# q and k of a fused attention and MLP-mixer kernel: transposes by DMA in place of transposes by TensorE

## The chip, the cores and the metric

The kernel runs on one core of a Trainium2 chip. The metric is the device time of one execution in microseconds (us), as the median of several runs. The kernel before takes 470.36 us (three runs, 468.58 to 470.69). A "slow" state of a run is kept apart; it appeared three times, in one run of the kernel before (635.32 us) and in two runs of e12_q_only, and these runs are in no comparison.

## The reference

The inputs are 8 batches of 12 heads, 448 rows, 64 columns. Attention with normalized q and k is followed by an MLP mixer over the 768 columns of all heads. Cut to what matters:

```python
q_n = q / (norm(q, axis=-1) + 1e-6)
k_n = k / (norm(k, axis=-1) + 1e-6)
attn = softmax(q_n @ k_n.T / tau)             # tau = 0.1
x = (attn @ v)  ->  (batch, 448, 768)
h = relu(x.T @ w_tok1) @ w_tok2               # mixes the 448 rows, 256 hidden
u = x + h.T
out = u + relu(u @ w_ch1) @ w_ch2             # mixes the 768 columns, 1536 hidden
```

## The kernel before

Two heads are one pair, so there are 48 pairs; three pairs are a half batch, which is what one set of loads of q, k and v brings. `scaled` divides q and k by their norms and writes them in fp16 as `qn` and `kn`, 112 partitions by 512 elements. The score matmul takes q and k with the 64 columns on the partitions (64x448 in its trace), so they are transposed first: `tpose` does it with 8 TensorE transposes into PSUM (to which this kernel's matmuls write) and one VectorE copy to `qk`.

The scores go to `psS`, a large PSUM tile with a single buffer (`ps2`, `bufs=1`); all other PSUM tiles share the four slots of pool `ps`. A pair has two score groups, 0 and 1, and ScalarE computes the exponential of each. So each score group waits until the exponential of the group before it has read `psS`. TensorE fills the time between score groups with mixer matmuls of the batch before (`feed`).

```python
ps  = ctx.enter_context(tc.tile_pool(name="ps",  bufs=4, space=PSUM))
ps2 = ctx.enter_context(tc.tile_pool(name="ps2", bufs=1, space=PSUM))
att = ctx.enter_context(tc.tile_pool(name="att", bufs=3))
# ... cut ...
    def load_qk(n, lo=0, hi=6):
        # ... cut: tiles qh, kh, vs of half n ...
        nc.sync.dma_start(out=half[n]["q"][...], in_=q[...])
        nc.sync.dma_start(out=half[n]["k"][...], in_=k[...])

    def scaled(i, dve_k=False):
        lo = 2 * NCH * (i % HP)
        for a, (nm, src) in enumerate(zip(("qn", "kn"), sides(i))):
            dst = pipe[i][nm] = att.tile([SC, NCH, 2, E], FP16, name=f"{nm}_{i}", tag=nm)
            eng = nc.vector if dve_k and a else nc.gpsimd
            # ... cut: dst = src * rn ...

    def tpose(i):
        st = pipe[i]
        pst = ps.tile([128, 2, NCH, SC], FP16, name=f"pst_{i}", tag="b")
        for a, src in enumerate((st["qn"], st["kn"])):
            for c in range(NCH):
                nc.tensor.transpose(pst[:, a, c, :], src[:, c], id16[:SC, :SC])
        qk = att.tile([128, 2, S], FP16, name=f"qk_{i}", tag="qk")
        nc.vector.tensor_copy(out=qk[:], in_=pst[:].rearrange("p a c s -> p a (c s)"))
        st["qk"] = qk

    def score(i, cg):
        # ... cut ...
        psS = ps2.tile([SC, 2, 2, 512], FP32, name=f"psS_{i}_{cg}", tag="s")
        for j in range(2):
            c = 2 * cg + j
            for hh in range(2):
                hb = hh * 64
                nc.tensor.matmul(psS[:, hh, j, 0:S], qk[hb:hb + 64, 1, c * SC:(c + 1) * SC],
                                 qk[hb:hb + 64, 0, :], start=True, stop=True)
        nc.scalar.activation(out=st["pt"][:, cg], in_=psS[:, :, :, 0:S], func=AF.Exp, scale=inv_tau)
# ... cut; the loop over the pairs:
        for i in range(NP_ALL + 1):
            # ... cut: loads, squares ...
            if i >= 4 and i + 2 < NP_ALL:
                scaled(i + 2)
            # ... cut ...
                if i:
                    score(i, 0)
                feed(quota * 0.3)
                if i:
                    pv(i - 1, 0)
                feed(quota * 0.2, 500.0)
                if i and i + 1 < NP_ALL:
                    tpose(i + 1)
                if i:
                    score(i, 1)
                feed(quota * 0.3)
                if i:
                    pv(i - 1, 1)
                feed(quota * 0.2)
```

The traces keep the order of these calls: on TensorE, in the kernel before, 47 of the 48 pairs have their transposes between the two score groups of one pair, where `tpose` is called (the first pair's come ahead of all scores).

## Time and profile before

| | before |
|---|---|
| time, median of 3 runs | 470.36 us |
| TensorE busy in the profiled run | 418.2 us of 468.7 |
| start-up, until the first mixer matmul | 69.0 us |
| mixer part, until the last score matmul | 333.5 us, TensorE idle 7.1 |
| rest | 66.2 us |

The stages in the table are read from the profile's busy times; the first lines are its page. The line of part 1 gives busy time, share of the span and instruction count by engine. In part 2 each digit is the busy share of one of 40 equal slices in tenths; PEclk is the TensorE clock that the throttle granted, also in tenths. The last line is part 4, the chain of work that ended last, by engine.

```profile
PE 418.2 (89%) x4136; PEld 257.6 (55%) x4136; DVE 219.1 (47%) x442; ACT 232.4 (50%) x262; POOL 219.0 (47%) x220
...
PE   0405879999999999999999999999999999999995
...
PEclk9999999999999999999999999999999999999999
DMA  9997999941496037630585056811200011001012
...
PE 84%; ACT 6%; DVE 4%; POOL 2%; issue 2%; DMA 1%; SPq 0%; ACTq 0%; POOLq 0%
```

After the start-up TensorE is at 9 in nearly every slice, its clock is full (0.99 or 1.00 in the stages below), and it holds 84% of the chain. In the start-up the PEclk row must not be trusted: the trace's clock records begin at 61.8 us, and the profile prints full clock where it has none. Until then one 65-column matmul of `psO` starts 55 ns after the one before it (median), and 32 ns in what is recorded as full clock; in the recorded half clock it is 55 ns too. So the start-up had the pace of half clock.

The busy times of the three stages of the kernel before follow. The columns are the window, its length, then busy time and instruction count of PE, PEld, DVE, ACT and POOL, then the mean granted TensorE clock, the DMA engines' busy share, and GB/s.

```profile
0.00:69.00 69.00, 30.70 (x317) 20.24 (x318) 37.37 (x64) 28.38 (x31) 51.93 (x60) 1.00 1.04 208
69.00:402.50 333.50, 326.38 (x3386) 200.86 (x3386) 170.25 (x355) 187.66 (x203) 167.05 (x161) 1.00 0.41 99
402.50:468.70 66.20, 61.13 (x436) 36.45 (x434) 11.44 (x23) 16.33 (x30) 0.00 (x0) 0.99 0.11 42
```

In the start-up the DMA engines are saturated (a busy share of 1.04, 208 GB/s), and TensorE, busy for 30.7 of 69 us, is not the limit.

A stretch of the timeline of the kernel before shows one pair in the mixer part. The columns are start, duration, engine, line, operation and tiles; a bracket at the end is the idle time before it and what released it.

```profile
202.23 0.36 PE L183 MATMUL pst_2758<-id_86,qn_2594 112*128 112x112 f16 x4
202.43 0.36 PE L183 MATMUL pst_2758<-id_86,kn_2596 112*128 112x112 f16 x4
202.43 0.54 ACT L261 ACTIVATE gt_1_2351<-psG_6_2750 128x448 f16<-128x448 f32 x1
...
202.82 0.62 DVE L185 COPY qk_2767<-pst_2758 128x896 f16<-128x896 f16 x1 [0.89 <-PE pst_2758 L183]
...
203.34 1.66 ACT L200 ACTIVATE pt_2723<-psS_1_2769 112x1792 f16<-112x1792 f32 x1 [0.37 <-PE psS_1_2769 L198]
...
205.06 0.58 PE L198 MATMUL psS_0_2815<-qk_2767 64*112 64x448 f16 x4 [1.14 <-ACT pt_2723 L200]
```

The eight transposes cost TensorE about half a microsecond (from the first one's start to the next matmul 0.49), the copy costs VectorE 0.62. The second exponential starts right after its score, the first score group of the next pair waits for this exponential (not for the transposes, which were done at 203.4), and TensorE loses 1.1 us. This pair is one of the worst: the waits of TensorE in the kernel before begin like this (waiting tile, what it waited for, us in total, times, longest):

```profile
PE pst_145 L183 <- POOL qn_141 L175: 11.7, 1, 11.7
PE psS_1_290 L198 <- ACT pt_251 L200: 10.6, 1, 10.6
...
PE psS_0_2815 L198 <- ACT pt_2723 L200: 1.1, 1, 1.1
```

The two long ones are in the start-up.

### The profile page before, as it was taken

The page shows a single profiled execution, that of the slowest core. Times are in us where ns is not written, and L with a number is a line of the kernel's source. Part 1 is how long each engine was busy: PE and PEld are TensorE (multiplying, and loading weights), DVE is VectorE, ACT ScalarE, POOL GpSimd, SP SyncE. Part 2 cuts the span into 40 slices and gives each one's busy share as a digit, 9 for nine tenths or more (in the row PEclk, how much of TensorE's full clock was granted, in tenths as well). Part 3 has the DMA queues.
Part 4 walks back from the last instruction along what each step waited for, and adds up shares of the span by engine and source line. Part 5 has one row for each costly group of instructions (what it writes and reads, how often), then busy time and mean ns, then how long its engine had stood idle before and what let it go on. Part 6 is the DMA issues. An engine that isn't in the chain of part 4 may idle for free.

```text
span 468.7 us, 9522 instructions
## 1 busy us (share of the span) xinstructions
PE 418.2 (89%) x4136; PEld 257.6 (55%) x4136; DVE 219.1 (47%) x442; ACT 232.4 (50%) x262; POOL 219.0 (47%) x220
## 2 busy tenths in 40 slices
PE   0405879999999999999999999999999999999995
PEld 0203546655655566656665666555655666556563
DVE  2448658455654455354645455445635343123000
ACT  2324664776457634675457543674467433520410
POOL 4599698586455644465283825373481300000000
PEclk9999999999999999999999999999999999999999
DMA  9997999941496037630585056811200011001012
GB/s 193 229 229 182 216 205 230 214 93 28 123 216 119 1 106 174 144 69 4 141 196 119 0 143 138 182 31 50 79 35 1 19 51 44 26 22 48 34 49 86
DMA packets 72841, 50.02 MB, mean 107 GB/s; under 512 B 44448, under 2 KB 68448, under 8 KB 72800
## 3 DMA queue, kind: packets, MB, share of 16 engines
q1 hardware_dynamic: 69408, 44.05, 39.7%
q0 software_dynamic: 3392, 5.37, 6.2%
q8 instruction: 32, 0.52, 0.5%
q14 instruction: 9, 0.07, 0.1%
HBM read 43.78 MB, written 11.01 MB: 117 GB/s over the span
## 4 chain that ended last, share of the span: by engine, by line
PE 84%; ACT 6%; DVE 4%; POOL 2%; issue 2%; DMA 1%; SPq 0%; ACTq 0%; POOLq 0%
DMA qh_105<-in_q_dram 1%; DVE kn_324 L175 1%; DVE ssq_118 L157 1%; ACT pt_630 L200 1%; ACT pt_482 L200 1%; ACT pt_1042 L200 1%; DVE ssq_126 L157 0%; POOL sq_207 L152 0%; PE psF_2_1_5429 L278 0%; PE psF_2_0_5377 L278 0%; PE psF_2_1_4787 L278 0%; PE psF_1_0_4581 L278 0%; PE psF_0_1_4513 L278 0%; PE psF_2_1_3968 L278 0%; PE psF_2_0_3897 L278 0%
## 5 line engine op out<-in xcount | busy, mean ns | idle before, releaser
L259 PEld LDWEIGHTS <-wc1t 128*128 128x128 f16 x576 | 51.5, 98 | 51.1 <-issue 9.8
L278 PEld LDWEIGHTS <-gt_2_3862 128*128 128x128 f16 x168 | 15.3, 98 | 12.5 <-issue 2.4
L278 PEld LDWEIGHTS <-gt_1_2351 128*128 128x128 f16 x168 | 15.4, 98 | 12.2 <-issue 2.4
L278 PEld LDWEIGHTS <-gt_0_804 128*128 128x128 f16 x168 | 15.5, 98 | 11.2 <-issue 1.4
L278 PEld LDWEIGHTS <-gt_3_5342 128*128 128x128 f16 x168 | 15.9, 98 | 9.6
L227 PEld LDWEIGHTS <-w1t 128*128 128x128 f16 x128 | 11.3, 100 | 8.6 <-issue 3.5
L183 PE MATMUL pst_145<-id_86,qn_141 112*128 112x112 f16 x4 | 0.6, 294 | 11.7 <-POOL qn_141 L175 11.7
L198 PE MATMUL psS_1_290<-qk_185 64*112 64x448 f16 x4 | 1.0, 574 | 10.6 <-ACT pt_251 L200 10.6
L198 PEld LDWEIGHTS <-qk_185 64*112 64x112 f16 x8 | 0.8, 176 | 13.0 <-issue 12.5
L284 DVE COPY ost_0_6031<-psF_0_0_6032 128x384 f32<-128x384 f32 x1 | 0.6, 558 | 15.2 <-PE psF_0_0_6032 L281 15.2
L164 ACT ACTIVATE rn_119<-ssq_118,tiny 112x16 f32<-112x16 f32 x3 | 0.9, 307 | 12.1 <-DVE ssq_118 L157 12.1
L183 PEld LDWEIGHTS <-qn_141 112*128 112x128 f16 x4 | 0.3, 129 | 11.6 <-POOL qn_141 L175 11.6
L175 POOL TENSOR_TENSOR qn_5044<-qh_4311,rn_4315 112x512 f16<-112x512 f32 x1 | 1.0, 1042 | 10.4 <-DVE rn_4315 L167 10.4
L164 ACT ACTIVATE rn_109<-ssq_108,tiny 112x16 f32<-112x16 f32 x3 | 0.9, 304 | 9.2 <-DVE ssq_108 L157 9.2
L175 DVE TENSOR_TENSOR kn_324<-kh_116,rn_119 112x512 f16<-112x512 f32 x1 | 4.7, 4685 | 0.0
L281 PEld LDWEIGHTS <-ut_3_5341 128*128 128x128 f16 x42 | 3.5, 98 | 1.8
L281 PEld LDWEIGHTS <-ut_0_803 128*128 128x128 f16 x42 | 3.5, 98 | 1.8
L281 PEld LDWEIGHTS <-ut_1_2350 128*128 128x128 f16 x42 | 3.5, 98 | 1.8
L281 PEld LDWEIGHTS <-ut_2_3861 128*128 128x128 f16 x42 | 3.5, 98 | 1.8
L175 POOL TENSOR_TENSOR qn_3954<-qh_3191,rn_3195 112x512 f16<-112x512 f32 x1 | 1.0, 1043 | 7.3 <-DVE rn_3195 L167 7.3
L198 PE MATMUL psS_0_400<-qk_365 64*112 64x448 f16 x4 | 1.0, 598 | 3.7 <-DVE qk_365 L185 3.7
L152 POOL TENSOR_TENSOR sq_2301<-qh_2033 112x512 f32<-112x512 f32 x1 | 1.0, 1041 | 6.9 <-DVE ssq_1701 L157 6.9
(1726 smaller groups left out, 1310.3 us busy)
## 6 DMA issues: line engine op xcount, KB each, us to landing
wc1t<-in_moe_w_ch_dram POOLq DMA_DIRECT2D x2, 1152.0 KB, 13.2
wc2t<-in_moe_w_ch_dram POOLq DMA_DIRECT2D x2, 1152.0 KB, 15.3
vs_107<-in_v_dram SPq DMA_DIRECT2D x1, 672.0 KB, 8.3
qh_115<-in_q_dram SPq DMA_DIRECT2D x1, 672.0 KB, 10.6
kh_116<-in_k_dram SPq DMA_DIRECT2D x1, 672.0 KB, 12.6
vs_117<-in_v_dram SPq DMA_DIRECT2D x1, 672.0 KB, 8.6
qh_123<-in_q_dram SPq DMA_DIRECT2D x1, 672.0 KB, 11.1
kh_124<-in_k_dram SPq DMA_DIRECT2D x1, 672.0 KB, 13.1
```

What stands on the lines that cost most here:

```text
L152: nc.gpsimd.tensor_mul(out=sq[:, a], in0=src, in1=src)
L157: nc.vector.tensor_reduce(out=half[i // HP]["ssq"][:, :, lo:lo + 2 * NCH], in_=pipe[i]["sq"][:], axis=AXX.X, op=ALU.add)
L164: nc.scalar.activation(out=rn, in_=ssq, func=AF.Ln, bias=tiny[:])
L175: eng.tensor_tensor(out=dst[:].rearrange("p c g e -> p g c e"), in0=src, in1=_bcast_free(rn, E), op=ALU.mult)
L183: nc.tensor.transpose(pst[:, a, c, :], src[:, c], id16[:SC, :SC])
L198: nc.tensor.matmul(psS[:, hh, j, 0:S], qk[hb:hb + 64, 1, c * SC:(c + 1) * SC], qk[hb:hb + 64, 0, :], start=True, stop=True)
L200: nc.scalar.activation(out=st["pt"][:, cg], in_=psS[:, :, :, 0:S], func=AF.Exp, scale=inv_tau)
L227: nc.tensor.matmul(psR[:], w1t[:, m, tt * 128:(tt + 1) * 128], x16[b][:, m, dh * DH:(dh + 1) * DH], start=(m == 0), stop=(m == 3))
L259: nc.tensor.matmul(psG[:], wc1t[:, dt, ct * 128:(ct + 1) * 128], ut[:, dt, span(b)], start=(dt == 0), stop=(dt == DT - 1))
L278: nc.tensor.matmul(psF[:], rows(gt, ct), wc2t[:, ct, dh * DH:(dh + 1) * DH], start=(ct == 0), stop=False)
L281: nc.tensor.matmul(psF[:, 128 * i:128 * (i + 1)], rows(ut, 3 * dh + i), id16[:], start=False, stop=(i == 2))
L284: nc.vector.tensor_copy(out=o[:, 0:DH], in_=psF[:])
```

## The change

The intent is to take 384 transposes off the busiest engine and 48 copies off VectorE. Each pair's q and k are transposed by one DMA transpose each, from SBUF to SBUF, issued on ScalarE's queue at the place of the old `tpose`. This is the whole diff:

```diff
     def tpose(i):
         st = pipe[i]
-        pst = ps.tile([128, 2, NCH, SC], FP16, name=f"pst_{i}", tag="b")
+        qk = att.tile([128, 2, S], FP16, name=f"qk_{i}", tag="qk")
         for a, src in enumerate((st["qn"], st["kn"])):
-            for c in range(NCH):
-                nc.tensor.transpose(pst[:, a, c, :], src[:, c], id16[:SC, :SC])
-        qk = att.tile([128, 2, S], FP16, name=f"qk_{i}", tag="qk")
-        nc.vector.tensor_copy(out=qk[:], in_=pst[:].rearrange("p a c s -> p a (c s)"))
+            nc.scalar.dma_start_transpose(out=qk[:, a].rearrange("p (c s) -> p c s", c=NCH),
+                                          in_=src[:].rearrange("p c g e -> p (c g e)"))
         st["qk"] = qk
```

Nothing else moves: on ScalarE the two issues stand between the exponential of score group 0 and that of score group 1 of the pair before.

## The prediction

> **What bounds the kernel now.** TensorE. The busy row gives PE 89%, ScalarE 50%, VectorE 47%. By stages: 0 to 69 us is a start-up in which PE is busy only 31 of 69 us and the DMA engines are saturated (GB/s row: about 210); from 69 to 416 us PE is busy 340 of 347 us and DMA 40%; then 53 us of output matmuls. The chain of waits is 84% PE.
>
> **What the change removes.** Per pair 8 transposes. In the timeline the next matmul starts 0.49 us after the first transpose, so about 0.45 us of PE per pair once the clock is up: 48 pairs make about 20 us, nearly all on the PE-bound path in the middle. Also 48 VectorE copies of 0.62 us (30 us), off the path, and one PSUM slot per pair.
>
> **What it adds.** 96 DMA transposes of 112x512 f16 (11 MB), issued in order on ScalarE between the first and second exponential of each pair. [...]
>
> **How much is on the path.** For the 42 pairs from 60 us on I read from the timeline the time between ScalarE being free for the issues and the next pair's first score matmul, which needs q and k transposed. It is 2.1 us in about nine pairs, 3.6 to 4.4 in most, up to 7.4. [...]29 of 42 pairs stall, together about 42 us. The second exponential, held up by 2 us, has 1.3 us of slack on average, and none in some 13 pairs where score and exponential already alternate; that is the same stall. Against it stand 20 us saved. The start-up pairs, short and beside saturated loads, lose about 8 us more. The build also shows ScalarE's and SP's DMAs sharing eight completion semaphores[...].
>
> **Prediction: 500 us, 464 to 580 in 8 of 10. Faster by over 2%: 0.12; within 2%: 0.17; slower by over 2%: 0.71.**
>
> **What would show it.** Right: no transposes on PE, PE busy down by about 20 us, VectorE by 30; score matmuls (first of each pair) waiting on the DMA of qk, in the waits view 30 to 60 us in total, and the ScalarE queue showing issues of about 1 us; the middle stage longer, PE share near 80%[...]. Exponentials later after their scores by 1 to 2 us.
>
> **What would make it wrong.** If an issue costs 0.6 us and lands in 2 us, the stalls are about 12 us, below the saving, and the time falls to about 460. [...] If loads and transposes hold each other up through the shared semaphores, the start-up grows by far more than 8 us.

The forecast's sum was 470 − 20 + 42 + 8 = 500 us. Passages are cut from it at the marks: how an issue and a landing were costed, a nearly serial case, a cause for a lower clock, and a wait of early transposes for loads. The costs were estimates, 1.0 us (0.5 to 1.6) for an issue and 2.7 us (2 to 4) from the second issue's end to the landing, so 4.7 us for a pair with its two issues; the 2 us by which the text has the second exponential held up are these two issues. The 42 us of waits came from setting these against the times read from the timeline; that 29 of 42 pairs stall is no more than this estimate.

## More of the kernel before

In the mixer part TensorE works 326.4 of 333.5 us, nearly all of it at full clock (3.0 us are recorded at half clock).

In the whole mixer part the waits for exponentials sum to 6.8 us and the waits for transposed tiles to nothing.

## The result, and the profile after

The changed kernel takes 595.01 us (median of 4 runs, 594.08 to 598.69), the kernel before 470.52 us (468.58 to 471.5) beside it. The ratio is 1.267 (95% interval 1.260 to 1.274). Ratios here are the mean time of one kernel's fast runs over that of the other's fast runs of the same rounds, so not quite the ratio of the quoted medians. Executions over 1.5% slower than the fastest of the same kernel are left out of the means. Both results are correct.

The page of the kernel after, with the same parts and the two largest DMA queues of part 3 (packets, MB, share of the 16 engines' span):

```profile
PE 437.7 (74%) x3752; PEld 250.8 (42%) x3752; DVE 192.4 (32%) x394; ACT 232.0 (39%) x262; POOL 219.1 (37%) x220
...
PE   0122465767785679769699959769699979999996
...
PEclk9999999787897898889899969879799979999999
DMA  9988979635136630364616921466415111310102
...
q1 hardware_dynamic: 69408, 44.05, 31.7%
q10 hardware_dynamic: 46080, 11.02, 11.2%
...
PE 36%; DMA 19%; POOL 15%; issue 9%; ACT 8%; ACTq 8%; DVE 4%; SPq 0%; POOLq 0%
```

The count of TensorE instructions fell by the 384 transposes, and VectorE's busy time fell by 26.7 us. But TensorE's busy time *rose*, from 418.2 to 437.7 us, with less work. PEclk says why: the clock is now below full in much of the middle (0.89 over the mixer part, against 1.00 before). Queue q10 is the transposes: 11 MB, in 46,080 packets, because each transpose moves 448 packets of 256 bytes and 32 of 4. The chain, which was 84% TensorE, is now spread over DMA, GpSimd, ScalarE's queue and others.

The same three stages of the kernel after, and two windows of equal work that are explained below:

```profile
0.00:93.10 93.10, 26.78 (x252) 16.39 (x252) 33.61 (x58) 29.16 (x32) 55.83 (x64) 1.00 0.96 187
93.10:526.20 433.10, 349.72 (x3067) 197.88 (x3066) 147.32 (x313) 186.47 (x201) 163.31 (x157) 0.89 0.44 94
526.20:592.50 66.30, 61.21 (x438) 36.53 (x436) 11.43 (x23) 16.39 (x30) 0.00 (x0) 1.00 0.11 42
...
263.50:267.50 4.00, 4.00 (x15) 1.90 (x14) 0.00 (x0) 1.66 (x1) 2.91 (x3) 0.50 0.01 2
268.80:270.90 2.10, 2.10 (x21) 1.32 (x18) 0.87 (x3) 0.00 (x0) 0.00 (x0) 1.00 0.74 205
```

The start-up is 24.1 us longer and the mixer part 99.6 us; the end is unchanged. In the mixer part TensorE is idle 83.4 us (before: 7.1).

The waits of TensorE in the kernel after, longest first:

```profile
PE psS_0_158 L196 <- DMA qk_145<-kn_143: 22.1, 1, 22.1
PE psS_0_368 L196 <- DMA qk_332<-kn_205: 11.8, 1, 11.8
...
PE psS_0_1577 L196 <- DMA qk_1502<-kn_1322: 7.0, 1, 7.0
...
PE psS_0_2267 L196 <- DMA qk_2192<-kn_1986: 5.5, 1, 5.5
...
PE psS_0_4022 L196 <- ACT pt_3938 L198: 3.2, 1, 3.2
```

The first two are in the start-up. In the mixer part 15 waits for the DMA of `qk` sum to 57.1 us, and 15 waits for an exponential sum to 23.7 us. The timeline of the kernel after shows one of each kind. First pair 22, where a load of q and k for a later half batch is issued at the same time, then a pair with no load near it:

```profile
251.79 1.20 ACTq L182 DMA_TRANSPOSE qk_2192<-qn_1984  x1
...
252.21 0.36 SPq L286 DMA_DIRECT2D out_dram<-ost_1_2075  x1
...
252.67 0.39 SPq L126 DMA_DIRECT2D qh_2252<-in_q_dram  x1
...
253.08 1.94 ACTq L182 DMA_TRANSPOSE qk_2192<-kn_1986  x1
253.15 4.45 SPq L128 DMA_DIRECT2D kh_2253<-in_k_dram  x1
...
255.36 1.66 ACT L198 ACTIVATE pt_2129<-psS_1_2195 112x1792 f16<-112x1792 f32 x1 [3.17 <-issue]
...
262.66 0.99 PE L196 MATMUL psS_0_2267<-qk_2192 64*112 64x448 f16 x4 [5.50 <-DMA qk_2192<-kn_1986]
...
263.58 4.02 PE L276 MATMUL psF_2_1_2273<-wc2t,gt_0_732 128*128 128x384 f16 x12
...
268.84 2.11 PE L276 MATMUL psF_3_0_2320<-wc2t,gt_0_732 128*128 128x384 f16 x12
...
421.07 0.72 PE L196 MATMUL psS_1_3976<-qk_3875 64*112 64x448 f16 x4
...
421.31 1.20 ACTq L182 DMA_TRANSPOSE qk_3973<-qn_3817  x1
...
422.61 1.23 ACTq L182 DMA_TRANSPOSE qk_3973<-kn_3819  x1
...
423.88 1.66 ACT L198 ACTIVATE pt_3938<-psS_1_3976 112x1792 f16<-112x1792 f32 x1 [2.17 <-DMA qk_3973<-qn_3817]
...
425.60 0.99 PE L196 MATMUL psS_0_4022<-qk_3973 64*112 64x448 f16 x4 [3.20 <-ACT pt_3938 L198]
```

Three things are to be read here.

- *The late landing* (a transpose has landed when the trace has the last update of its completion semaphore). For pair 22 the first issue starts at 251.79 and the score that needs both transposes can start only at 262.66, 10.9 us later. The trace has the second transpose land 10.8 us after the first issue's start; the pair whose landing was least disturbed took 3.7 us. The trace's packet records show 224 transpose packets served in the half microsecond from 253.0, and then 2 to 67 per half microsecond until 258.0: first beside packets of 3072 bytes, which are a store of the output (issued at 252.21), and from 255.0 on beside the 256-byte packets of the load of q. So the slow stretch begins beside a store, before the load.
- *The held exponential.* In the second pair the score group ends at 421.8, but the exponential starts at 423.88, because ScalarE's queue has two issues of 1.2 us each ahead of it. The next score needs this exponential's buffer and starts at 425.60, after 3.2 us of TensorE idle time. (The transposes landed at about 425.0, half a microsecond before the exponential's end.)
- *The clock.* The twelve `psF` matmuls that follow the 5.5 us wait take 4.02 us; the same twelve a few microseconds later take 2.11. The two windows in the fence before say that the granted clock was 0.50 and 1.00. Half-clock stretches in the mixer part of this trace last 3.41 or 6.83 us.

### The profile page after: what moved, and what is told of

It is laid out like the page before. It is cut to its first block, busy times and chain, and to the rows that moved or that the text cites. A ratio compares the mean times of both kernels' runs of the same rounds, so it can differ in the third digit from the quotient of the medians.

```text
span 592.5 us, 8929 instructions
## 1 busy us (share of the span) xinstructions
PE 437.7 (74%) x3752; PEld 250.8 (42%) x3752; DVE 192.4 (32%) x394; ACT 232.0 (39%) x262; POOL 219.1 (37%) x220
## 3 DMA queue, kind: packets, MB, share of 16 engines
q10 hardware_dynamic: 46080, 11.02, 11.2%
## 4 chain that ended last, share of the span: by engine, by line
PE 36%; DMA 19%; POOL 15%; issue 9%; ACT 8%; ACTq 8%; DVE 4%; SPq 0%; POOLq 0%
ACTq L182 8%; DMA qk_332<-kn_205 2%; DMA qk_696<-kn_566 2%; DMA qk_1502<-kn_1322 2%; DMA qk_800<-kn_644 1%; DMA qk_2060<-kn_1882 1%; DMA qk_394<-kn_227 1%; DMA qk_3475<-kn_3297 1%; DMA qk_3156<-kn_2968 1%; DMA qk_1378<-kn_1218 1%; DMA qh_105<-in_q_dram 1%; DMA qk_2460<-kn_2261 1%; DMA kh_1874<-in_k_dram 1%; DMA qk_3875<-kn_3676 1%; DMA qk_1085<-kn_949 1%
## 5 line engine op out<-in xcount | busy, mean ns | idle before, releaser
L257 PEld LDWEIGHTS <-wc1t 128*128 128x128 f16 x576 | 55.8, 105 | 61.8 <-issue 27.4
L276 PEld LDWEIGHTS <-gt_1_2175 128*128 128x128 f16 x168 | 16.4, 103 | 14.5 <-issue 6.4
L276 PEld LDWEIGHTS <-gt_0_732 128*128 128x128 f16 x168 | 16.5, 104 | 13.7 <-issue 5.7
L276 PEld LDWEIGHTS <-gt_2_3590 128*128 128x128 f16 x168 | 15.3, 98 | 12.4 <-issue 3.4
L276 PEld LDWEIGHTS <-gt_3_4974 128*128 128x128 f16 x168 | 15.9, 98 | 9.6
L196 PE MATMUL psS_0_158<-qk_145 64*112 64x448 f16 x4 | 1.0, 598 | 22.1 <-DMA qk_145<-kn_143 22.1
L196 PEld LDWEIGHTS <-qk_145 64*112 64x112 f16 x8 | 0.7, 187 | 24.4 <-DMA qk_145<-kn_143 22.1
L196 PE MATMUL psS_0_368<-qk_332 64*112 64x448 f16 x4 | 1.0, 598 | 11.8 <-DMA qk_332<-kn_205 11.8
L196 PE MATMUL psS_1_266<-qk_168 64*112 64x448 f16 x4 | 1.0, 574 | 8.3 <-ACT pt_235 L198 8.3
L196 PEld LDWEIGHTS <-qk_168 64*112 64x112 f16 x8 | 0.7, 182 | 14.6 <-issue 8.2
L198 ACT ACTIVATE pt_367<-psS_0_368 112x1792 f16<-112x1792 f32 x1 | 1.7, 1663 | 11.9 <-PE psS_0_368 L196 11.9
L196 PE MATMUL psS_0_1577<-qk_1502 64*112 64x448 f16 x4 | 1.0, 596 | 7.0 <-DMA qk_1502<-kn_1322 7.0
L196 PEld LDWEIGHTS <-qk_332 64*112 64x112 f16 x8 | 0.7, 181 | 12.7 <-DMA qk_332<-kn_205 11.9
L175 POOL TENSOR_TENSOR qn_3674<-qh_2959,rn_2963 112x512 f16<-112x512 f32 x1 | 1.0, 1041 | 12.9 <-DVE rn_2963 L167 12.9
L175 POOL TENSOR_TENSOR qn_182<-qh_105,rn_109 112x512 f16<-112x512 f32 x1 | 1.5, 1547 | 11.5 <-DVE rn_109 L167 11.5
L175 POOL TENSOR_TENSOR qn_2259<-qh_1562,rn_1566 112x512 f16<-112x512 f32 x1 | 1.0, 1041 | 12.3 <-DVE rn_1566 L167 12.3
L175 POOL TENSOR_TENSOR qn_4692<-qh_4007,rn_4011 112x512 f16<-112x512 f32 x1 | 1.0, 1042 | 11.9 <-DVE rn_4011 L167 11.9
L175 POOL TENSOR_TENSOR qn_435<-qh_123,rn_127 112x512 f16<-112x512 f32 x1 | 1.0, 1042 | 11.4 <-DVE rn_127 L167 11.4
L196 PE MATMUL psS_0_3682<-qk_3607 64*112 64x448 f16 x4 | 1.0, 598 | 5.8 <-DMA qk_3607<-kn_3401 5.8
## 6 DMA issues: line engine op xcount, KB each, us to landing
wc1t<-in_moe_w_ch_dram POOLq DMA_DIRECT2D x2, 1152.0 KB, 15.1
```

The source lines that it names most:

```text
L175: eng.tensor_tensor(out=dst[:].rearrange("p c g e -> p g c e"), in0=src, in1=_bcast_free(rn, E), op=ALU.mult)
L257: nc.tensor.matmul(psG[:], wc1t[:, dt, ct * 128:(ct + 1) * 128], ut[:, dt, span(b)], start=(dt == 0), stop=(dt == DT - 1))
L276: nc.tensor.matmul(psF[:], rows(gt, ct), wc2t[:, ct, dh * DH:(dh + 1) * DH], start=(ct == 0), stop=False)
```

## The experiments

The expectations name their theories themselves. In short, the first one was that most of the loss is TensorE waiting for transposes that land late, with the low clock that follows each wait. Its rival was that most of it comes even if nobody waits for the data, from the issues on ScalarE and from the extra traffic. Another rival was that the clock is the cause rather than a follower of the waits. All runs below gave a correct result unless it is said that the wrong result is on purpose. Each time is compared with the kernel before on the same chip, with a median of 470.6 to 470.7 us in its fast runs.

"Half clock" in what follows is the time in the mixer part in which the trace records a granted clock of 0.5. In the kernel after, e2, e4, e5, e6, e11 and e12 the records begin only 2.2 to 5.2 us into the mixer part; that first bit is not counted (in the kernel after and in e5 the matmuls have the pace of half clock there; in the kernel after, a 384-column `psR` matmul starts 320 ns after the one before it, as in its recorded half clock, and 162 at full clock).

### Issue and transfer, with nobody waiting (e1_shadow)

TensorE transposes are kept, and the DMA transposes are added, into a tile that nothing reads.

```diff
  # in before's tpose, after the copy:
+        sh = att.tile([128, 2, S], FP16, name=f"sh_{i}", tag="sh")
+        for a, src in enumerate((st["qn"], st["kn"])):
+            nc.scalar.dma_start_transpose(out=sh[:, a]..., in_=src[:]...)
```

> The kernel before, TensorE transposes and copies kept, plus the same 96 DMA transposes on ScalarE's queue into a tile that nobody reads. Theory A (the loss is the next score matmul waiting for a transpose that lands late, and the TensorE clock halving after each such wait): with nobody waiting only ScalarE's 2.5 us of issue per pair is left, so 470 to 505 us, hardly any half clock, although transposes issued beside loads still take 6 to 12 us to land. Rival B (the 2.5 us of issue ahead of the second exponential is itself the loss): 560 us or more.

Measured: 511.0 us, ratio 1.086 (1.082 to 1.091). This is just above the range of the first theory and far below that of its rival: neither number was right, the issues with their transfers cost more than the first theory allowed, and half clock was 30.7 us where hardly any was expected. The mixer part of this run:

```profile
74.80:444.90 370.10, 338.80 (x3387) 206.72 (x3386) 171.04 (x356) 185.54 (x203) 166.53 (x160) 0.96 0.55 114
```

It is 36.6 us longer than before's, with TensorE idle 31.3 us, of which 30.5 wait for exponentials. So the issues between two exponentials, with their transfers, cost about 40 us of the 125 even if nobody waits for the data; the rest appears only when somebody does.

### No loads beside the transposes (e2_after_noload, e3_before_noload)

From the fourth half batch on, the loads of q, k and v are left out and old tiles are used again. The result is wrong. The second kernel is the control, with TensorE transposes.

```diff
     def load_qk(n, lo=0, hi=6):
+        if n >= 3:      # reuse half n-3's q and k, half n-2's v, and return
+            half[n] = dict(q=half[n - 3]["q"], k=half[n - 3]["k"], vs=half[n - 2]["vs"], ...)
+            return
     def load_v(n):
+        if n >= 3:
+            return
```

> The changed kernel, but q, k and v are loaded only for the first three half batches and used again for the others (wrong result on purpose). Theory A with the cause of the lateness named (the loads of q and k share the 16 DMA engines with the transposes): from pair 12 on every pair lands about 3.7 us after its first issue, as the undisturbed ones of the changed kernel do; waits on transposes in the mixer part fall from about 83 us to under 35, half clock from 92 us to under 40; total 495 to 530, the start-up still about 93. Rival B (issue cost) and rival C (a transpose is slow by itself): landing and time stay, 575 to 600.

> The control for it: the kernel before with the same loads left out (wrong result on purpose). All theories: TensorE-bound in the middle, so 460 to 470; if it fell by more than 10 us, part of the gain of the other run would be the loads' own.

Measured: 522.61 us (1.111, 1.105 to 1.117) for the change without loads, and 471.85 us (1.002, 0.998 to 1.006) for the control, 2 us above its range. Loads are worth nothing to the kernel before and 72 us to the changed one, 65 of them in the mixer part. That loads and transposes share the DMA engines agrees with the packet records of the kernel after: up to 29 packets of the queue of loads and stores (q1) are in flight at once, up to 31 of the transposes' (q10), and never over 31 of all queues. The start-up, expected at about 93 us, fell to 83.1. Of the 38 pairs from pair 10 on, 34 now land within 5 us. In the mixer part, the waits for transposes fall from 57.1 to 6.9 us and half clock from 92.2 to 37.5 us. This is the summary of TensorE's waits over the whole run:

```profile
PE psS L203 <- ACT pt L205: 51.5, 36, 8.9
PE psS L203 <- DMA qk<-kn: 43.9, 5, 21.2
```

The second line is now mostly the start-up (37 of 43.9), which keeps the loads of the first three half batches. What is left in the mixer part is the first line: 32.2 us for exponentials, nearly the shadow's 30.5.

### The transposes one step earlier (e4_early, e10_before_early)

`scaled` and `tpose` run one pair earlier, so that the data has a whole pair more time to land. The loads and the issuing queue stay. The second kernel makes the same moves with TensorE transposes.

```diff
-            if i >= 4 and i + 2 < NP_ALL:
-                scaled(i + 2)
+            if i >= 3 and i + 3 < NP_ALL and (i + 3) % HP:
+                scaled(i + 3)          # for (i + 3) % HP == 0 at the end of the step, after its norms
-                if i and i + 1 < NP_ALL:
-                    tpose(i + 1)
+                if i + 2 < NP_ALL:
+                    tpose(i + 2)       # and 4 buffers for qk
```

> The changed kernel with the transposes of a pair issued one pair earlier (and q and k scaled one pair earlier), so each has about 8 us more to land; ScalarE still pays the issue. Theory A: waits on transposes nearly vanish after the start-up, half clock under 35 us, 480 to 530 us. Rival B: the exponentials are held up as before, 560 or more.

> Control: the kernel before with the same earlier scaling and earlier (TensorE) transposes. TensorE-bound, so within 1.5% of before, 465 to 476 us, perhaps a few us less in the start-up.

Measured: 520.15 us (1.105, 1.099 to 1.111) and 479.17 us (1.018, 1.016 to 1.021). The mixer part of the early kernel:

```profile
79.20:452.20 373.00, 329.00 (x3066) 190.76 (x3066) 147.32 (x315) 184.92 (x203) 165.99 (x160) 0.94 0.59 113
```

It is 373.0 us, against 368.2 without loads: two different ways of having the data there in time give nearly the same mixer part. Transposes are waited for 8.3 us, exponentials 35.5. Half clock was 44 us, more than the 35 that was expected. The control was a miss: the earlier order costs 8.6 us where TensorE transposes, which now wait for `qn` and `kn` from GpSimd (6.1 us in the mixer part). So the earlier order is no gain in itself.

### The issues on SyncE's queue (e5_sp, e6_early_sp)

Only the queue changes. The second kernel has the earlier order as well.

```diff
-            nc.scalar.dma_start_transpose(out=qk[:, a]..., in_=src[:]...)
+            nc.sync.dma_start_transpose(out=qk[:, a]..., in_=src[:]...)
```

> The changed kernel with the transposes issued from SyncE's queue instead of ScalarE's, not earlier. So far two causes are seen: late landing beside loads, and 2.5 us of issue ahead of the second exponential, which delays the next score through the one score buffer. This run takes the second away and leaves the first, or makes it worse, since the transposes now also stand behind the loads in one queue: waits on transposes 80 us or more, waits for exponentials back near the 26 us of before; 530 to 590 us. If issue on ScalarE were all, about 460.

> Both taken away: SyncE's queue and one pair earlier. If the two causes are all there is, the mixer part runs at its 333 us of before less some 18 us of TensorE transposes, with little half clock: 315 to 325 us; with a start-up still some 5 to 15 us longer the total is 450 to 475. If the transposes cost something else (DMA bandwidth, SBUF), it stays over 490.

Measured: 487.53 us (1.035, 1.031 to 1.039) and 481.79 us (1.024, 1.022 to 1.026). The first was a large miss: the range was 530 to 590. (The "26 us of before" in its text is the waits for exponentials of the whole run; in the mixer part they are 6.8.) The second was a miss too: 450 to 475 us was expected, with a mixer part of 315 to 325, and that part took 329.1, with one wait of 8.7 us for a transpose about 20 us after its beginning. The reason for the first is a second effect of the queue. SyncE's queue has no compute ahead of the issue, so a transpose is issued as soon as `qn` and `kn` are scaled and the queue's own loads and stores are issued; the median time from the first issue to the score that needs it rises from 6.5 to 8.8 us, which is enough in most pairs. (With the earlier order it is about 14 us in all variants.) The mixer parts of the run with the queue alone and of that with the earlier order as well:

```profile
89.90:416.60 326.70, 311.29 (x3066) 183.00 (x3066) 146.97 (x316) 187.36 (x203) 166.33 (x160) 1.00 0.61 127
...
86.00:415.10 329.10, 312.62 (x3066) 183.75 (x3066) 146.84 (x316) 187.43 (x203) 166.07 (x160) 0.99 0.62 130
```

In the first of them TensorE is busy 311.3 us, with no half clock on record, in the same instructions that took 349.7 us in the kernel after. Waits for exponentials are back at 7.4 us, as before (6.8), and waits for transposes at 7.4.

Between e4_early and e6_early_sp only the queue differs and the data mostly arrives in time in both (waits for transposes 8.3 and 8.7 us): 520.2 against 481.8, so the queue costs 38 us there, and the waits for exponentials are 35.5 against 7.4. That agrees with the shadow's 40.

What keeps these kernels above the kernel before is the start-up: 89.9 and 86.0 us against 69.0.

### TensorE in the start-up, DMA later (e7_hybrid_sp, e8_hybrid_sp_noearly, e9_hybrid_lateearly)

Pairs 0 to 9 are transposed by TensorE, later ones by DMA on SyncE's queue. e7 has the earlier order throughout, e8 nowhere, e9 from pair 10 on.

```diff
     def tpose(i):
+        if i < 10:
+            # before's eight TensorE transposes and the copy
+        else:
+            # nc.sync.dma_start_transpose of qn and of kn
```

> As the run before it, but pairs 0 to 9 keep TensorE's transposes, since the loads fill the DMA engines during the start-up. Start-up near 69 us again, mixer part 316 to 326, so 448 to 465 us: faster than both kernels. If not under 465, something in the mixer part is not understood.

> TensorE's transposes for pairs 0 to 9, after that DMA transposes on SyncE's queue at their old place, nothing earlier. The control with earlier TensorE transposes lost 8 us, mostly waits for qn from GpSimd, so leaving the order alone should help; against that some pairs again wait for a transpose. Start-up 69 us, mixer part 315 to 326: 450 to 462 us. If the earlier issue is what makes SyncE's version work, it is 470 or more.

> The same, but from pair 10 on the scaling and the transposes come one pair earlier; the start-up is exactly that of before. Start-up 69, mixer part 313 to 320, total 446 to 458 us, 0 to 8 us under the run before it.

Measured: 456.89 us (0.971, 0.969 to 0.972), 465.40 us (0.990, 0.987 to 0.992) and 456.49 us (0.971, 0.968 to 0.973). The start-up is back at 70.6, 69.4 and 69.0 us. e8 missed its range by 3 us: without the earlier order 7.5 us of waits for transposes stay. The mixer part of e9:

```profile
69.00:388.60 319.60, 311.84 (x3082) 184.26 (x3082) 147.86 (x318) 187.32 (x203) 166.36 (x161) 0.99 0.63 130
```

TensorE is busy 311.8 us instead of 326.4 and idle 7.8 instead of 7.1. So the saving that the change was made for exists (14.6 us of TensorE time in the mixer part), and it comes out as 13.9 us of mixer part when nothing gives it back. This version is faster than both kernels, by 2.9% against before.

### The clock by itself (e11_warm)

The kernel after, with 391 matmuls of no use added at the places where TensorE waited, as many as would about fill each wait at full clock. If the low clock does harm beyond the waits, more work should take less time.

```diff
+WARM = {8: 27, 9: 13, 10: 12, ...}     # 22 pairs, 391 matmuls in all
+                if i in WARM:            # ahead of score(i, 0)
+                    psW = ps.tile([128, S], FP32, name=f"psW_{i}", tag="b")
+                    for _ in range(WARM[i]):
+                        nc.tensor.matmul(psW[:], id16[:], wc1t[:, 0, 0:S], start=True, stop=True)
```

> The changed kernel with 391 idle matmuls (73 us of TensorE work at full clock, into an unread PSUM tile) put ahead of those score matmuls that waited over 1 us in its profile, as many as fit into each wait. If the halved clock after a wait is a cost of its own, half clock falls from 92 us to under 50 and the time falls by 10 to 35 us although TensorE does more: 560 to 585 us. If the waits are the whole cost, it stays at 595 or rises.

Measured: 568.6 us (1.210, 1.204 to 1.216). Its mixer part:

```profile
94.40:505.10 410.70, 388.24 (x3458) 220.88 (x3457) 146.92 (x313) 185.98 (x201) 161.91 (x156) 1.00 0.47 99
```

With about 74 us of extra work (an estimate: 391 matmuls at the 189 ns from one 448-column `psG` matmul to the next at full clock in the kernel after) the kernel is 26 us faster than the kernel after, and half clock falls from 92.2 to 3.4 us. The clock is a cost of its own, but not the first cause: with the low clock nearly gone, 98 us of the loss remain, because the filler occupies the waits and does not remove them.

Seven traces together (before, after, e1, e2, e4, e5, e12) say which waits are followed by half clock, counting waits of TensorE in the mixer parts that begin at full clock: from 0.8 to 1.5 us none of 30; from 1.5 to 2.5 us 8 of 22; from 2.5 to 3.0 us 17 of 21; above 3.0 us 23 of 23. In the trace of the kernel after alone these are none of 2, 2 of 2, 5 of 7 and 12 of 12.

### One of the two transposes (e12_q_only)

q by DMA on ScalarE's queue, k by TensorE.

```diff
+        nc.scalar.dma_start_transpose(out=qk[:, 0]..., in_=st["qn"][:]...)
+        # k: four TensorE transposes and a copy of half the size
```

> Half of the change: q by one DMA transpose per pair on ScalarE's queue, k by TensorE. One issue of 1.2 us holds the second exponential up by less than half as much (0.4 us of it is idle time anyway) and lands by 2.4 us when undisturbed. If hold-up and late landing both scale with what is issued, 495 to 545 us; over 560 would mean that the cost is per pair, not per transpose.

Measured: 508.04 and 515.62 us in the two fast runs (1.088, 1.078 to 1.098); two more runs, of 516.25 and 519.84 us, count as slow. It is as expected, and it does not scale simply: half of the transposes cost 41 us, all of them 124. In the mixer part, transposes are waited for 18.0 us instead of 57.1, exponentials 11.1 instead of 23.7, and half clock is 17.1 us instead of 92.2. Less waiting (TensorE is idle 30.9 us instead of 83.4) goes with less half clock here.

### All runs side by side

Times are medians (of e12_q_only, the mean of its two fast runs); the other columns are us of the profiled run; waits are those of the mixer part. A dash was not taken.

| kernel | time | start-up | mixer part | PE busy | PE idle | half clock | waits for transposes by DMA | waits for exponentials |
|---|---|---|---|---|---|---|---|---|
| before | 470.5 | 69.0 | 333.5 | 326.4 | 7.1 | 3.0 | 0 | 6.8 |
| after | 595.0 | 93.1 | 433.1 | 349.7 | 83.4 | 92.2 | 57.1 | 23.7 |
| e1_shadow | 511.0 | 74.8 | 370.1 | 338.8 | 31.3 | 30.7 | 0 | 30.5 |
| e2_after_noload | 522.6 | 83.1 | 368.2 | 327.9 | 40.3 | 37.5 | 6.9 | 32.2 |
| e3_before_noload | 471.9 | 68.0 | 333.4 | 326.2 | 7.1 | 2.7 | 0 | – |
| e4_early | 520.2 | 79.2 | 373.0 | 329.0 | 44.0 | 44.4 | 8.3 | 35.5 |
| e10_before_early | 479.2 | 69.6 | 340.9 | 327.9 | 13.0 | 2.6 | 0 | 6.8 |
| e5_sp | 487.5 | 89.9 | 326.7 | 311.3 | 15.4 | 0.0 | 7.4 | 7.4 |
| e6_early_sp | 481.8 | 86.0 | 329.1 | 312.6 | 16.5 | 6.8 | 8.7 | 7.4 |
| e7_hybrid_sp | 456.9 | 70.6 | 318.9 | 310.2 | 8.7 | 0.0 | 0 | – |
| e8_hybrid_sp_noearly | 465.4 | 69.4 | 327.7 | 312.2 | 15.6 | 3.0 | 7.5 | 7.4 |
| e9_hybrid_lateearly | 456.5 | 69.0 | 319.6 | 311.8 | 7.8 | 3.5 | 0 | 7.4 |
| e11_warm | 568.6 | 94.4 | 410.7 | 388.2 | 22.5 | 3.4 | 13.2 | 7.1 |
| e12_q_only | 511.8 | 81.0 | 359.0 | 328.1 | 30.9 | 17.1 | 18.0 | 11.1 |

## Why the prediction was wrong

The direction was right, and the size was far off: 500 us with a range up to 580, and 595 measured. The prediction's sum was 470 − 20 + 42 + 8. Against it stand the spans of the two profiled runs, 592.5 − 468.7 = 123.8 us. The clock's term is the busy time of the kernel after less that of e5_sp, 349.7 − 311.3: the same instructions, in a run without half clock on record.

| term | predicted, us | measured, us |
|---|---|---|
| TensorE transposes removed, mixer part | −20 (all of the middle) | −15.1 (326.4 to 311.3) |
| waits of TensorE in the mixer part | +42 | +76.3 (idle 7.1 to 83.4) |
| the same work at half clock | not in the sum | +38.4 |
| start-up | +8 | +24.1 |
| end | 0 | +0.1 |
| sum | +30 | +123.8 |

**Right: what is removed.** TensorE work fell by 418.2 − 399.3 = 18.9 us over the whole kernel, taking the sum of its busy time from e5_sp, the run without half clock. The prediction said 20. VectorE fell by 26.7; predicted 30.

**Right, and a little low: the issue.** The author's estimate was 1.0 us (0.5 to 1.6), on a basis that no run shows; measured 1.20 us and 1.23 to 1.28 us, and up to 2.1 us beside loads.

**Right in kind: the place of the stall.** The prediction expected 29 of 42 pairs to stall, together for 42 us. In the mixer part the first score group of 30 pairs waits (over 0.15 us), 15 times for the DMA of `qk` and otherwise, but for one, for an exponential; so the number was nearly right, and the length, 83 us together with one wait of a second group, was not. The issues do hold up the second exponential. The prediction took the held exponential for the same stall as the transposes; with no load near, the exponential is the later of the two (in pair 37 it ends 4.2 us after the first issue's start, and the transposes land after 3.7). The shadow shows the second effect alone (+40 us), and e4_early against e6_early_sp shows it again (38 us).

**Wrong, the step that failed first: the landing, estimated at 2.7 us (2 to 4) from the second issue's end, for all pairs alike.** The landing is not one number. In an undisturbed pair the landing is 1.16 us after the second issue's end (3.68 us after the first one's start), less than predicted. In the mixer part's pairs that take 7 to 12 us to land, all of them beside loads, it is 3.7 to 9.5 us. Of the 38 pairs from pair 10 on, 16 take more than 5 us; 13 of these have packets of q, k or v in flight, two only a store of the output, one neither. A 112x512 transpose here landed 2.4 us after its issue's start at best, 4.0 in the median, and 14.1 at worst. e2_after_noload shows that the loads are most of what makes it late: without them the median landing of a pair is 3.75 us, waits for transposes fall from 57.1 to 6.9 us, and the time falls by 72 us, while the control does not move. The prediction looked at the DMA row of the mixer part as a mean of 40% and missed that the loads come in bursts, at the same few pairs.

**Wrong, a missing term: the clock.** The prediction named a lower clock only as possible in the start-up. The traces agree with a lower clock there, but it is no difference between the kernels: up to the first clock record, at 61.8 us before and 97.1 after, the matmuls of both have the pace of half clock (55 ns from one `psO` matmul to the next, 32 or 33 afterwards). The mixer part's clock fell to 0.89, which it did not foresee. In the seven traces all 23 waits above 3.0 us were followed by half clock, and 17 of 21 from 2.5 to 3.0 us. By the estimate about nine waits were to be 2.6 us long (4.7 us needed, 2.1 there) and the others 0.3 to 1.1; by the count above most of these nine would bring half clock. But that count was made after the prediction; the trace that the prediction was made from, of the kernel before, has no such wait in its mixer part (the longest is 1.14 us), so nothing there showed this term.

**Wrong, a size: the start-up.** Its two longest waits for transposes are 22.1 and 11.8 us, beside saturated loads (the DMA engines' busy share is 0.96 in this start-up; the first counts from the start of the trace; 11.8 us of it pass before the first transpose is issued); the stage grew by 24.1 us, not 8. e7, e8 and e9 take them away by giving pairs 0 to 9 back to TensorE and have the start-up of before.

**Not a cause, as far as the trace shows: the shared completion semaphores.** In the trace of the kernel after ScalarE's transposes and SyncE's loads and stores report on the same eight semaphores (100, 101, 102, 104, 105, 107, 108 and 109). The prediction had early transposes wait for loads because of it; no run shows such a wait. The 82 semaphore waits recorded directly ahead of transposes on ScalarE's queue, from 23.2 us on, are 17 ns in the median and 38 at most; waits of up to 6.6 us are recorded elsewhere on this queue, so a long one would show.

**Why 75 us and 107 us do not add.** Making the transposes earlier takes 75 us off the kernel after, changing the queue 107, both 113. The queue change does two things (no held exponential, and an earlier issue), and the second is the same cure as the earlier order. The cause is thus: two issues of 1.2 us between two exponentials that a single score buffer couples to TensorE; an issue that waits for ScalarE's turn and then has no time to spare when loads stretch the landing; and the clock, at which the work after the longer waits takes nearly twice as long (4.02 against 2.11 us).

**Still open.** Which of the transfers delays a transpose most was not tried apart. The packet records of the kernel after give an order, which is no test: from pair 10 on, seven pairs beside nearly the whole load of q landed after 6.7 to 11.1 us, four beside a load of k or v and a whole store of the output after 7.7 to 8.7, and five beside a store alone after 4.4 to 6.2. In the 38 us between e4_early and e6_early_sp, the part of the waits and that of the clock were not tried apart. A second score buffer, which might let the exponential come late, was not tried; no run shows whether PSUM has room for it.

## What to carry to other kernels

Before moving work from a compute engine to a DMA, find for each use the time between the earliest possible issue and the first reader, and compare it with the landing time beside the bursts of loads (here 7 to 12 us for the pairs that landed late beside loads), not the landing time alone (3.7 us). Put the issue on a queue whose engine has nothing in its order that others wait for (here worth 107 us of 595), and issue at the place where the source becomes ready. When a change leaves waits on a TensorE-bound kernel that are as long as those that half clock followed here (8 of 22 from 1.5 to 2.5 us, 40 of 44 longer ones), count the half-clock work that follows each wait as well as the wait.
